# Attention and experts on one core: attention as one written order of pieces, sub-blocks of 24 queries, v in 16 transfers a batch

## The chip, the core and the metric

The kernel runs on one core of a Trainium2 chip. The core has a matmul engine (PE; its weight loads are shown apart as PEld), three engines for elementwise work (DVE, ACT, POOL), a queue engine (SP) that issues most transfers, and 16 DMA engines that carry them out. Each engine takes its instructions strictly in the order in which the program gives them. The metric is the device time of one execution in microseconds, the median of the runs.

## What is computed

Eight batches of eight heads go through two attentions, one over the sequence averaged by fours and one over a band of seven keys around each query. Their sum, seen as 4608 rows of 512 numbers, goes through a layer of eight experts, of which each row takes one.

```python
q_d, k_d, v_d = (x.reshape(B, H, Sd, 4, D).mean(axis=3) for x in (q, k, v))   # B, H, S, D = 8, 8, 576, 64
out_up = np.repeat(sm_attn(q_d, k_d, v_d), 4, axis=2)
mask = np.abs(pos[:, None] - pos[None, :]) < 4
out_local = softmax(where(mask, scale * q @ k.T, -1e9)) @ v
x = (out_up + out_local).transpose(0, 2, 1, 3).reshape(B * S, H * D)
e_idx = argmax(x @ w_gate + modality_bias[modality_id], axis=1)
out[mask_e] = gate_w * (relu(x[mask_e] @ w1[e]) @ w2[e])                      # for each expert e
```

## The kernel before

**Attention** runs over 32 head pairs (8 batches of 4). For a pair, PE transposes q and k (tile tp, 12 transpositions, L238), ACT and DVE copy them out (qT, kT) and the averages are taken (qd, kd, d). The banded scores are small matmuls (sc, L275): the 576 queries are cut into sub-blocks of SUB = 26 with a window of 32 keys each, four sub-blocks to a row of tiles, so the last sub-blocks are partial or missing (46 of 48 in all for a pair). DVE takes maximum and difference (lm, le), ACT the exponential, POOL the normalization (L306, L317), DVE transposes 32x32 blocks (lt, L309) and ACT copies them into Pw (L312). The averaged attention goes through scd, de, pdt and PdT. The values matmuls (avd L334, avl L344) and the final addition on DVE (L352) write X, which holds a batch's rows.

**Loads.** `load_qk` (L188) fetches q and k for two pairs in eight transfers of 144 KB. `load_v` (L199) fetches the windows of v for a whole batch in 23 transfers, one for each sub-block over all eight heads; the first has 29 rows, the last 7, the others 32. `load_vg` (L213) fetches v again for averaging, once for each pair, and POOL averages it (L221, L222). All go through SP's queue in program order; vw has two buffers, so a batch's v waits until the values matmuls two batches back have read theirs.

**Router.** After each batch PE computes the logits (lg, lgt), DVE chooses the expert and the place of each row, POOL scatters the entries (tab, L445, 4 or 5 transfers a batch) and PE, ACT and SP write the rows to DRAM (xr, R, xs; L459, L460, L462). The scatters of the batches after the fifth come after the attention loop.

**Experts.** Units of 256 rows: entries and rows are gathered (tg, xg), transposed and split into two parts (xh, xl), as the weights are (whi, wlo, L612, L613), and multiplied (L677, L724). Two units on rows of the first batches start before the router has ended.

**The order.** A loop over steps n (L764) calls, for each n, the loads and `pre` of pair n, `softmax` of pair n-2, `scores` of pair n-1 and `av` of pair n-3. Within what this gives, the scheduler of the build (L934) places each engine's instructions by its own estimates; priorities are raised for the router's last batch. Eighteen dummy matmuls (tile bz, L95) keep PE active, 12 at the start and 6 at step 4.

Of the kernel before, what the change touches and what calls it, by code (L numbers as in the profile page):

```python
# [7 lines left out]
F32 = mybir.dt.float32  # L8
# [14 lines left out]
SUB, WIN = 26, 32  # L23
# [3 lines left out]
KT = PAD + S - 4 + WIN  # L27
# [10 lines left out]
EARLY = 576 * EB  # L38
# [3 lines left out]
LAG = 3  # L42
N0,N1,N2 = (2,3,4)
PV = 0
AN = 2
LEAD = 8
ST = 1
NPW = 3
SP0 = ()
NS1 = 33  # L50
HOLD = 14
NHOLD = 20
HIP = 1
GO = 1
LS = 1
VD = 0
NCE = (2,1,1)
BZ = (0,0,0,0,6)


class Consts:
    def __init__(s, tc, pool, psum):
# [25 lines left out]
        nc.vector.memset(s.mask[64:96, NB - 1, 4 + PAD : WIN], NEG)  # L88
# [8 lines left out]
    def load(s, tc, pool, work, rows, mid, bias, w_gate):  # L97
# [3 lines left out]
        nc.sync.dma_start(s.wg[:, :, 0:NE], w_gate.rearrange("(j p) e -> p j e", p=128))  # L101
        s.mi = rows.tile([128, DM], F32, name="R", bufs=3)[:36, :256].bitcast(I32)
# [41 lines left out]
    def biases(s, tc, pool, work, rows, psum):  # L144
# [11 lines left out]
        t1 = rows.tile([128, DM], F32, name="R", bufs=3)[:, : 36 * NE].rearrange("p (t e) -> p t e", e=NE)  # L156
# [6 lines left out]
class Attention:  # L163
    def __init__(s, tc, ctx, ectx, C, psum, q, k, v):
# [7 lines left out]
        s.QK, s.V, s.VG = {}, {}, {}  # L172
        s.vw = [(s.ld, s.one)[j].tile([128, NB, H, D], F32, name=f"vw{j}", bufs=1) for j in range(2)]
        s.kT = [s.ld.tile([128, KT], F32, name=f"kT{j}", bufs=1) for j in range(2)]
        s.Pw = [s.one.tile([128, 2 * NB, 4, SUB], F32, name=f"Pw{j}") for j in range(NPW)]
        s.clear(0)

    def clear(s, j):

        nc = s.nc  # L180
        if j < 2:
            nc.vector.memset(s.kT[j][:, 0:PAD], 0.0)
            nc.vector.memset(s.kT[j][:, S + PAD :], 0.0)
            nc.vector.memset(s.vw[j][0:32, 0], 0.0)
            nc.vector.memset(s.vw[j][64:96, NB - 1], 0.0)
        (nc.vector if j == 0 else nc.gpsimd).memset(s.Pw[j], 0.0)

    def load_qk(s, b, half):  # L188
# [4 lines left out]
        for g in range(2):  # L193
            for t, src in ((qt, s.q), (kt, s.k)):
                for a in range(2):
                    nc.sync.dma_start(t[:, g, :, a], src[b, 4 * half + 2 * g + a].rearrange("(j p) d -> p j d", j=6))
        s.QK[b, half] = (qt, kt)

    def load_v(s, b):  # L199
        nc = s.nc  # L200
        vd = s.wk.tile([72, H, 2, D], F32, name="vd")
        vw = s.vw[b % 2]
        s.V[b] = (vw, vd)

        for i in range(NB):
            for j in range(4):
                lo = BLK * i + SUB * j - PAD
                k0, k1 = max(lo, 0), min(lo + WIN, S)
                if lo + PAD < S:
                    nc.sync.dma_start(vw[32 * j + k0 - lo : 32 * j + k1 - lo, i],  # L210
                                      s.v[b, :, k0:k1].rearrange("h p d -> p h d"))

    def load_vg(s, b, hp):  # L213
# [725 lines left out]
```

## Time and profile before

| | |
|---|---|
| median of 3 runs | 798.09 us (797.21 to 799.65) |
| profiled execution | 799.32 us, span 797.6 us |
| mean granted clock of PE | 0.927 |
| DMA | 150.00 MB, mean 188 GB/s |
| chain that ended last | issue and DMA of the last output, below 1% of the span |

The profile gives busy time for each engine, the granted clock of PE and the DMA's share over time, and rows in order of time with the idle time ahead of an instruction and what ended it, in brackets. The chain that ended last breaks off after the last output transfers, so the argument has to come from stretches of the span: attention lies in the first 350 us, the experts behind it.

### The profile page before, as it was taken

To read this page: it belongs to the slowest core of one execution; us is meant where nothing else is said; L and a number is where in the kernel's file an instruction comes from. 1 tells how busy PE (TensorE), PEld (TensorE's weight loads), DVE (VectorE), ACT (ScalarE), POOL (GpSimd) and SP (SyncE) were. 2 spreads that over 40 slices of the span, in tenths; PEclk is the share of its full clock that TensorE was granted. 3 is DMA by queue.
4 is the path that set the end of the run, shared out by engine and by line. 5 is a ranking of instruction groups with operands and counts; after the bars stand their busy time and mean duration, and the time that the engine had idled before them with its cause. 6 is when DMAs were issued, how large, how long until landed. Compare 5 with 4: busy or idle time off the path is not lost. (4 is left out here: it accounts for less than half of the span.)

```text
span 797.6 us, 20726 instructions
## 1 busy us (share of the span) xinstructions
PE 739.1 (93%) x8185; PEld 616.6 (77%) x8185; DVE 469.4 (59%) x957; ACT 426.5 (53%) x882; POOL 319.2 (40%) x362
## 2 busy tenths in 40 slices
PE   8488999899989988899799999999999999999995
PEld 5366767576767666778699888999998899999884
DVE  7534757574657667858476555556555555655520
ACT  4534657474747356855466555545555554555520
POOL 5525565665574658323353333233222333222000
PEclk9685989897989679999989999999999999999998
DMA  8769967577868597334889766677666667666500
GB/s 143 149 135 179 202 132 201 104 177 138 209 125 210 98 235 189 110 108 176 283 275 321 253 207 227 213 249 237 229 227 220 216 225 233 224 217 231 186 13 18
DMA packets 205075, 150.00 MB, mean 188 GB/s; under 512 B 132683, under 2 KB 171631, under 8 KB 204976
## 3 DMA queue, kind: packets, MB, share of 16 engines
q1 hardware_dynamic: 196720, 129.43, 59.5%
q0 software_dynamic: 8256, 19.22, 6.8%
q8 instruction: 65, 1.06, 0.6%
q14 instruction: 34, 0.28, 0.2%
HBM read 129.40 MB, written 19.47 MB: 187 GB/s over the span
## 5 line engine op out<-in xcount | busy, mean ns | idle before, releaser
L613 DVE TENSOR_TENSOR wlo<-raw,whi 128x1024 fp32r<-128x1024 f32 x130 | 160.2, 1245 | 130.4 <-ACT whi L612 120.7
L612 ACT CAST whi<-raw 128x1024 fp32r<-128x1024 f32 x130 | 134.7, 1049 | 120.2 <-PE l L677 54.3
L677 PE MATMUL l<-xh,whi 128*128 128x256 f32 x488 | 138.8, 286 | 0.7 <-ACT xh L660 0.7
L677 PE MATMUL l<-xh,wlo 128*128 128x256 f32 x488 | 138.4, 284 | 0.0
L677 PE MATMUL l<-xl,whi 128*128 128x256 f32 x488 | 138.3, 284 | 0.0
L728 POOL DMA_INDIRECT out_dram<-o,tg x37 | 40.9, 1105 | 173.3 <-ACT o L727 127.7
L724 PE MATMUL l<-wlo,hh 128*128 128x512 f32 x256 | 100.4, 393 | 0.0
L724 PE MATMUL l<-whi,hl 128*128 128x512 f32 x256 | 100.4, 393 | 0.0
L724 PE MATMUL l<-whi,hh 128*128 128x512 f32 x256 | 98.7, 397 | 0.0
L677 PEld LDWEIGHTS l<-xh,whi 128*128 128x128 f32 x488 | 93.3, 192 | 2.5 <-ACT xh L660 1.1
L677 PEld LDWEIGHTS l<-xl,whi 128*128 128x128 f32 x488 | 93.4, 191 | 0.6
L677 PEld LDWEIGHTS l<-xh,wlo 128*128 128x128 f32 x488 | 93.3, 191 | 0.2 <-issue 0.2
L275 PEld LDWEIGHTS sc<-kT,qT 64*26 64x26 f32 (+1 forms) x2944 | 40.7, 104 | 36.6 <-issue 27.3
L275 PE MATMUL sc<-kT,qT 64*26 64x32 f32 (+1 forms) x2944 | 60.7, 199 | 8.9 <-issue 8.4
L626 POOL DMA_INDIRECT tg<-tab,midx x33 | 38.1, 1154 | 75.3 <-DMA out_dram<-o,tg 69.5
L680 DVE SCALAR_TENSOR_TENSOR hl<-l,hh 128x512 fp32r<-128x512 f32 x72 | 49.3, 685 | 24.8 <-ACT hh L679 24.8
L312 ACT COPY Pw<-lt 32x312 f32<-32x312 f32 x128 | 57.7, 451 | 10.4 <-DVE lt L309 8.3
L636 POOL DMA_INDIRECT xg<-xs,tg x37 | 43.3, 1170 | 47.6 <-DMA tg<-tab,midx 29.7
L679 ACT ACTIVATE hh<-l 128x512 fp32r<-128x512 f32 x72 | 42.8, 594 | 32.4 <-PE l L677 29.2
L724 PEld LDWEIGHTS l<-whi,hl 128*128 128x128 f32 x256 | 48.1, 188 | 10.7 <-issue 0.5
L724 PEld LDWEIGHTS l<-wlo,hh 128*128 128x128 f32 x256 | 48.0, 188 | 10.8
L724 PEld LDWEIGHTS l<-whi,hh 128*128 128x128 f32 x256 | 48.1, 188 | 10.6 <-issue 0.5
(203 smaller groups left out, 1444.1 us busy)
## 6 DMA issues: line engine op xcount, KB each, us to landing
raw<-in_moe_w_dram SPq DMA_DIRECT2D x152, 512.0 KB
vw<-in_v_dram SPq DMA_DIRECT2D x168, 64.0 KB
qt<-in_q_dram SPq DMA_DIRECT2D x64, 144.0 KB
kt<-in_k_dram SPq DMA_DIRECT2D x64, 144.0 KB
vg<-in_v_dram SPq DMA_DIRECT2D x32, 288.0 KB
xs<-R SPq DMA_DIRECT2D x36, 256.0 KB
xg<-xs,tg POOLq DMA_INDIRECT x37
out_dram<-o,tg POOLq DMA_INDIRECT x37
```

The costliest lines, as they stand in the source:

```text
L275: nc.tensor.matmul(p[32 * j : 32 * j + q1 - q0, i, :], qT[r, q0:q1], kT[r, q0 : q0 + WIN], start=False, stop=(i == NB - 1), skip_group_che ...
L312: nc.scalar.copy(Pw[r, :, j, :SUB], eT[r, :, :SUB])
L612: nc.scalar.copy(hi, raw)
L613: nc.vector.tensor_tensor(lo, raw, hi.bitcast(F32), op=ALU.subtract)
L626: nc.gpsimd.indirect_dma_start(out=T[:, h, :], out_offset=None, in_=s.tab[:, :], in_offset=bass.IndirectOffsetOnAxis(ap=idx[:, u, h : h + ...
L636: s.gathered = nc.gpsimd.indirect_dma_start(out=R[:, h, :], out_offset=None, in_=s.xs[:n, :], in_offset=bass.IndirectOffsetOnAxis(ap=T[:, ...
L677: nc.tensor.matmul(p[:, f, :], a[:, k, fs], x[:, k, :], start=(k == 0 and i == 0), stop=(k == 3 and i == 2))
L679: nc.scalar.activation(hh[:, 2 * c : 2 * c + 2, :], p, AF.Relu)
L680: nc.vector.scalar_tensor_tensor(hl[:, 2 * c : 2 * c + 2, :], p, 0.0, hh[:, 2 * c : 2 * c + 2, :].bitcast(F32), op0=ALU.max, op1=ALU.subtract)
L724: nc.tensor.matmul(p, a[:, f, hs], x[:, f % 2, :], start=(f == 0 and i == 0), stop=(f == 7 and i == 2))
L728: nc.gpsimd.indirect_dma_start(out=s.out[:, :], out_offset=bass.IndirectOffsetOnAxis(ap=T[:, h, 0:1], axis=0), in_=o, in_offset=None, boun ...
```

## The change

- All pieces of attention and of the router's work for the first seven batches become methods for one engine each. A table, PHASE, gives each piece a time in units of a pair's period (W0 at 11.2 for a batch's last piece); all calls are sorted by pair or batch number plus that time and written out in that order, under a manual schedule in which the build keeps the order as written.
- SUB is 24, so 24 sub-blocks cover the 576 queries exactly. A batch's windows of v are loaded in four parts of two heads, each in four transfers of 32 rows by 12 blocks; the transfers of a part are calls in the sorted order. Windows may now reach into the neighbouring head, where the band mask leaves nothing.
- q and k for two pairs come in four transfers instead of eight, except the first. Heads are paired two apart, with the matching order in the router's weights and the row copies. vg has three buffers and is loaded three pairs ahead.
- The six dummy matmuls at step 4 are gone. Normalization is on POOL for all pairs. The 64 columns of an even batch that belong to the next row block are kept in a tile `late` and copied by POOL.
- The scatters of every batch but the last stand in the sorted order, one call each. The expert weights' loading and splitting are separate calls. The last batch's router and the experts are scheduled by the build, as before.

```diff
-SUB, WIN = 26, 32
+SUB, WIN = 24, 32
-LAG = 3
-BZ = (0,0,0,0,6)
+PHASE = {
+    "tpq1": 0.0047, "tpk1": 0.0434, "qT1": 0.3244, "kT1": 0.4158, "tpq0": 0.4432, "qT0": 0.5686, "tpk0": 0.7338,
...
+}
...
-        for i in range(NB):
-            for j in range(4):
-                lo = BLK * i + SUB * j - PAD
-                k0, k1 = max(lo, 0), min(lo + WIN, S)
-                if lo + PAD < S:
-                    nc.sync.dma_start(vw[32 * j + k0 - lo : 32 * j + k1 - lo, i],
-                                      s.v[b, :, k0:k1].rearrange("h p d -> p h d"))
+        for j in (0, 2, 1, 3):
+            lo = S * H * b + SUB * j - PAD
+            n0, n1 = NB * 2 * part, NB * 2 * part + NB * 2
...
+            nc.sync.dma_start(vw[32 * j : 32 * j + 32, n0:n1],
+                              vf[lo + n0 * BLK : lo + n1 * BLK].rearrange("(n x) d -> x n d", x=BLK)[:32])
...
+            for nm, p in P.items():
+                f, i = (nm[:-1], int(nm[-1])) if nm[-1].isdigit() and nm not in ("ch1", "ch2") else (nm, 0)
+                if f in batch:
+                    for b in range(B - 1):
+                        call(4 * b + p, getattr(ro, parts.get(f, f)), b, i)
+                else:
+                    for n in range(N):
+                        call(n + p, values if f == "X" else getattr(at, parts.get(f, f)), n, i)
+            for b in range(B):
+                if b + 1 < B:
+                    for j in range(4):
+                        call(4 * b - 1 + used + 0.3 + 0.4 * j, at.load_v, b + 1, j)
+            for h in range(2, N // 2):
+                call(2 * h - 3 + last + 0.25, at.load_qk, h // 2, h % 2)
+            for n in range(3, N):
+                call(n - 3 + P["vt"] + 0.25, at.load_vg, n)
...
+            calls.sort(key=lambda x: x[:2])
+            with tc.manual_schedule():
+                for x in calls:
+                    if x[0] < free:
+                        x[2](*x[3])
```

Where instructions move is shown at three places. First SP's queue in mid-attention, around the load of v for an even batch, before:

```order
L196 DMA kt<-in_k_dram 96x6x64 x2
L210 DMA vw_153<-in_v_dram 29x8x64
L210 DMA vw_153<-in_v_dram 32x8x64 x4
L215 DMA vg<-in_v_dram 72x2x512
L210 DMA vw_153<-in_v_dram 32x8x64 x17
L210 DMA vw_153<-in_v_dram 7x8x64
L215 DMA vg<-in_v_dram 72x2x512
L462 DMA xs<-R 128x512 x2
L196 DMA qt<-in_q_dram 96x6x64 x2
L196 DMA kt<-in_k_dram 96x6x64 x2
```

and after the change, the load for an even batch as well:

```order
L230 DMA vw_153<-in_v_dram 32x12x64 x4
L236 DMA vg<-in_v_dram 72x2x512
L209 DMA qt<-in_q_dram 96x12x64 x2
L209 DMA kt<-in_k_dram 96x12x64 x2
L230 DMA vw_153<-in_v_dram 32x12x64 x8
L559 DMA xs<-R 128x512
L230 DMA vw_153<-in_v_dram 32x12x64 x4
L236 DMA vg<-in_v_dram 72x2x512 x2
L209 DMA qt<-in_q_dram 96x12x64 x2
```

The block of 23 v transfers with one vg in it has become groups of four and eight, with vg, q, k and a store of rows between them.

Second POOL's queue where a batch's entries are scattered (tab) in mid-attention, before (vt and vd average v, le and de are normalized, d and kd average k):

```order
L253 TENSOR_TENSOR kd<-d_3857 128x72x2
L445 DMA tab<-ig,si 36864x2 x2
L221 TENSOR_TENSOR vt<-vg 72x512
L445 DMA tab<-ig,si 36864x2 x3
L306 TENSOR_TENSOR le<-le,zr 128x384
L317 TENSOR_TENSOR de<-de,zr 128x432
L221 TENSOR_TENSOR vt<-vg 72x512
```

and after:

```order
L564 DMA tab<-ig,si 36864x2
L357 TENSOR_TENSOR le<-le,zr 128x384
L250 TENSOR_TENSOR vd<-vt 72x256
L564 DMA tab<-ig,si 36864x2
L243 TENSOR_TENSOR vt<-vg 72x512
L564 DMA tab<-ig,si 36864x2
L285 TENSOR_TENSOR d_3138<-kT_156 128x288
L361 TENSOR_TENSOR de<-de,zr 128x432
L290 TENSOR_TENSOR kd<-d_3138 128x72x2
L357 TENSOR_TENSOR le<-le,zr 128x384
```

The five scatters around one vt stand ahead of the normalization before; after the change each scatter has other work on at least one side, and the normalization comes between them.

Third PE's queue within a pair in mid-attention, before (sc are the banded scores, scd and avd belong to the averaged attention, avl are the values, xr the router's rows):

```order
L275 MATMUL sc<-kT_155,qT 26x32 x20
L334 MATMUL avd<-PdT,vd 64x144 x2
L344 MATMUL avl<-Pw_159,vw_154 64x104 x6
L459 MATMUL xr<-ident,X 128x128 x4
L334 MATMUL avd<-PdT,vd 64x144 x2
L459 MATMUL xr<-ident,X 128x128 x4
L238 MATMUL tp<-ident,qt 128x96 x3
L275 MATMUL sc<-kT_155,qT 26x32 x12
L275 MATMUL sc<-kT_155,qT 4x32
L238 MATMUL tp<-ident,qt 128x96 x3
L344 MATMUL avl<-Pw_159,vw_154 64x104 x4
L344 MATMUL avl<-Pw_159,vw_154 64x78 x2
```

and after:

```order
L258 MATMUL tp<-ident,kt 128x96 x3
L304 MATMUL sc<-kT_156,qT 24x32 x48
L393 MATMUL avd<-PdT,vd 64x144 x4
L258 MATMUL tp<-ident,qt 128x96 x3
L258 MATMUL tp<-ident,kt 128x96 x3
L331 MATMUL scd<-kd,qd 64x144 x6
L408 MATMUL avl<-Pw_157,vw_153 64x96 x12
L258 MATMUL tp<-ident,qt 128x96 x3
```

Before, scores, values and transpositions of several pairs are mixed in small pieces that differ from pair to pair; after the change each piece is whole and the sequence repeats from pair to pair.

656 lines of the change are left out of this document (350 added, 306 removed), and 11 rows, old and new, of the table PHASE.

## Prediction

> **What bounds the kernel now.** I start with the page's busy shares and clock row.
>
> ```profile
> PE 739.1 (93%) x8185; PEld 616.6 (77%) x8185; DVE 469.4 (59%) x957; ACT 426.5 (53%) x882; POOL 319.2 (40%) x362
> PEclk9685989897989679999989999999999999999998
> ```
>
> TensorE is busy 93% of the span, and from the twentieth slice on, in the experts, it is full at full clock. The change leaves the experts' instructions as they are, so what can move is the first 350 us, where the clock row falls to 5 and 6 again and again. The table of 20 us stretches shows how (from: to, length; busy us and number of instructions of PE, PEld, DVE, ACT, POOL; granted clock; DMA share; GB/s):
>
> ```profile
> 120.00:140.00 20.00, 19.13 (x394) 14.24 (x392) 14.70 (x50) 13.66 (x41) 11.50 (x14) 1.00 0.78 205
> 140.00:160.00 20.00, 16.64 (x269) 12.14 (x265) 10.62 (x32) 10.12 (x29) 12.80 (x17) 0.83 0.55 97
> 160.00:180.00 20.00, 17.99 (x421) 13.74 (x417) 15.38 (x48) 14.55 (x48) 12.13 (x16) 1.00 0.79 185
> 180.00:200.00 20.00, 18.64 (x274) 13.41 (x275) 9.40 (x25) 8.29 (x27) 11.81 (x15) 0.75 0.70 132
> 200.00:220.00 20.00, 19.84 (x390) 14.65 (x390) 13.83 (x49) 13.84 (x42) 10.50 (x14) 1.00 0.85 214
> 220.00:240.00 20.00, 17.41 (x275) 12.16 (x274) 11.05 (x35) 9.00 (x27) 13.31 (x17) 0.83 0.66 122
> 240.00:260.00 20.00, 19.35 (x429) 14.38 (x429) 14.15 (x47) 13.70 (x45) 10.30 (x13) 1.00 0.85 209
> 260.00:280.00 20.00, 19.29 (x227) 12.91 (x226) 12.41 (x41) 7.55 (x22) 13.70 (x17) 0.66 0.56 100
> ```
>
> Good and bad stretches alternate, one of each to a batch. The good ones (120, 160, 200, 240) hold 394+421+390+429 = 1634 matmul records in 80 us, 20.4 a us, with PE busy 76.3 of 80 and the clock at 1.00. The bad ones hold 1045, 13.1 a us, at 0.66 to 0.83, and there the DMA moves 97 to 132 GB/s instead of about 200. What a head pair costs comes from one longer stretch, first all instructions, then those on tile tp, of which PE has 12 for each pair:
>
> ```profile
> 100.00:260.00 160.00, 147.40 (x2740) 107.76 (x2739) 99.63 (x310) 93.97 (x289) 94.13 (x117) 0.90 0.73 162
> ```
> ```profile
> 100.00:260.00 160.00, 29.34 (x198) 19.83 (x198) 14.90 (x34) 13.33 (x34) 0.90 0.73 162
> ```
>
> 198/12 = 16.5 pairs in 160 us: **9.70 us a pair**, 166 records each. At the good stretches' 20.4 a us a pair would be 8.14 us. DVE, ACT and POOL have 6.0, 5.7 and 5.7 us of work a pair: none is near the bound. So what makes the bad half? The transfer queue's rows in order of time, and its waits:
>
> ```profile
> 12.80 15.05 SPq L210 DMA_DIRECT2D vw<-in_v_dram  x23
> 28.73 0.87 SPq L196 DMA_DIRECT2D qt<-in_q_dram  x2
> 39.80 15.22 SPq L210 DMA_DIRECT2D vw<-in_v_dram  x21
> ```
> ```profile
> 226.79 15.21 SPq L210 DMA_DIRECT2D vw<-in_v_dram  x23
> 242.10 0.98 SPq L215 DMA_DIRECT2D vg<-in_v_dram  x1
> 261.39 0.42 SPq L215 DMA_DIRECT2D vg<-in_v_dram  x1
> ```
> ```profile
> SPq L210 <- PE avl L344: 19.7, 9, 7.6
> ```
>
> The 23 v transfers of a batch hold the queue about 15.2 us, 0.66 us each for 64 KB, the rest of a batch's transfers 19.7 us more (242.10 to 261.81), and v also waits up to 7.6 us for the values matmuls that free its buffer, with q and k of later pairs queued behind it. 15.2 + 19.7 us and waits of a few us are the batch's 38.8 us (four times 9.70): **the in-order queue sets the period**, not an engine. And v is slow on its own account:
>
> ```profile
> 2.00:13.00 11.00, 10.26 (x169) 6.35 (x167) 8.79 (x33) 2.88 (x9) 6.60 (x19) 1.00 1.29 208
> 14.00:28.00 14.00, 9.03 (x274) 6.67 (x271) 11.27 (x34) 11.79 (x42) 5.55 (x8) 0.94 0.45 102
> ```
>
> With q and k queued the DMA gave 208 GB/s at a share of 1.29; with v queued without a gap, 102 at 0.45. [...]
>
> PE pays for the queue directly and through POOL:
>
> ```profile
> 34.20 1.19 PE L238 MATMUL tp<-ident,qt 96*128 96x96 f32 x6 [9.38 <-DMA qt<-in_q_dram]
> 42.81 2.74 PE L95 MATMUL bz<-dummy 128*128 128x512 bf16 x6
> 62.38 1.19 PE L238 MATMUL tp<-ident,qt 96*128 96x96 f32 x6 [6.51 <-DMA qt<-in_q_dram]
> ```
> ```profile
> 225.58 0.24 PE L268 MATMUL sc<-mask,identb 128*128 128x192 bf16 x1 [2.50 <-DVE le L279]
> ```
> ```profile
> 216.87 1.01 POOL L445 DMA_INDIRECT tab<-ig,si  x1 [0.74 <-DVE si L440]
> 223.17 0.97 POOL L445 DMA_INDIRECT tab<-ig,si  x1 [0.30 <-issue]
> 224.17 0.84 POOL L306 TENSOR_TENSOR le<-le,zr 128x384 f32<-128x384 f32 x1
> ```
>
> At 34.20 and 62.38 PE had waited 9.38 and 6.51 us for q. At 225.58 it had waited 2.50 us for the scores' subtraction on DVE: POOL's normalization (224.17) stood behind five scatters in a block from 216.87 on, and the later DVE work behind that.
>
> **The change, part by part.** *The start.* Sizes are in the page's section 6, k's like q's:
>
> ```profile
> vw<-in_v_dram SPq DMA_DIRECT2D x168, 64.0 KB
> qt<-in_q_dram SPq DMA_DIRECT2D x64, 144.0 KB
> vg<-in_v_dram SPq DMA_DIRECT2D x32, 288.0 KB
> ```
>
> The first transfer PE runs dry on is q for pair 4. After the change there stand ahead of it, in KB: q and k of the first four pairs, 16x144 = 2304; vg, 3x288; v, 16x96 (32 rows of 12 blocks of 64 numbers); some 60 for the router; and pair 4's two q transfers themselves, which now bring two pairs at once, 288 each. That is 5340 KB, 5.47 MB. At 208 GB/s from 2 us on it is there at 28.3 us, against 34.20. PE's work up to there is done at about 25 us as before, so a wait of some 3 us stays and the clock falls; I charge 3 us for that and for the six dummy matmuls (2.74 us at 42.81) that go: their loss cannot cost more than the half clock did after 62.38, and their absence gains at most 2.74. Pairs 4 and 5 at the period below: pair 6 starts at 28.3+3+17 = 48.3 instead of 62.38. Its q is behind k of pair 4, the table's fill, two vg and four v, 2.46 MB with itself, 11.8 us, so it is there at 40 and nothing waits. **Gain 14.1 us.**
>
> *The period.* v goes in pieces of a quarter batch between q, k and vg, each due when its buffer is free, so nothing stands behind a wait. What the queue needs a batch: 19.7 us as before, plus v. v is bounded by 1.57 MB at 208 GB/s, 7.6 us, and by the old pace per byte, 15.2 us x 1536/1416 KB = 16.5 us: 27 to 36 us. I take the lower end, near which q and k run, since all transfers but the run's first and last are now 32 full rows, with no more 29 and 7 rows in every batch; q and k come in half as many transfers with the same bytes. PE needs 4x8.14 = 33 us and becomes the bound. To 8.14 us I add 0.35 for waits of a strict order, from these rows:
>
> ```profile
> L460 ACT COPY R<-xr 128x512 f32<-128x512 f32 x36 | 20.3, 589 | 15.8 <-PE xr L459 8.7 <-PE scd L286 2.2 <-PE tp L238 1.7
> L388 ACT COPY LT<-lg 128x256 f32<-128x256 f32 (+1 forms) x16 | 6.4, 398 | 17.3 <-PE lg L386 17.2
> ```
>
> In one pair of each four two R and two LT copies now stand ahead of the copies that the values matmuls wait for: 2x589+2x398 = 2.0 us, of which I let a quarter of ACT's slack (8.1-5.7 = 2.4 us a pair) take 0.6, since the rest of the slack lies elsewhere in the pair; 1.4/4 = 0.35. Together **8.5 us**. The scores' 46 blocks become 48 (4 records of 166, at most 0.2 us a pair), the values matmuls are 96 instead of 104 wide (8% of 24 records, about -0.1): nothing, with ends of -3 and +5 us over the run. POOL gains the copies of 64 leftover columns, four in all, and the first two pairs' normalizations; it has 2.8 us of slack a pair. The scatters, now one at a time, no longer make a block, so the stall at 225.58 goes; last in line is then PE itself. In the last batch SP's reading of the early experts' numbers stands between two pieces of v, with the rest of v, xs and vg behind it; v is wanted three periods later, 25 us, which covers that. The row copies' new pattern and three more small loads at the start I cost at nothing: ACT and SP have the slack named. How far pairs run:
>
> ```profile
> L238 PE MATMUL tp<-ident,qt x192: 243/246/422, 6.0 to 309.6; 96*128 96x96 f32 x192
> ```
> ```profile
> 351.68 0.71 PE L344 MATMUL avl<-Pw,vw 128*64 128x104 f32 x12
> ```
>
> The last q transposition stands at 309.6; from pair 6 on 25.4 periods, 9.73 us each. At 8.5: 48.3 + 25.4x8.5 = 264.2. **Gain 31.3 us there, 45.4 in all.**
>
> *The end of attention.* From 309.6 to the last values matmul (351.68) are 42 us, in which the first expert's work is mixed in before and after. The order hardly differs there, so I cost it at nothing, between -6 (less waiting in the drain) and +8 (weights of the first expert late). After it the routing of the last batch, scatters, reading of the table and gather follow one another as before; PE runs dry at the end of that chain:
>
> ```profile
> 60.00:80.00 20.00, 17.52 (x210) 12.33 (x210) 8.51 (x22) 8.84 (x25) 11.32 (x14) 0.51 0.95 179
> 392.00:400.00 8.00, 2.99 (x12) 1.88 (x11) 4.37 (x5) 4.61 (x7) 4.41 (x4) 0.68 0.93 313
> ```
>
> 3.0 us of 8 are busy there. That gap moves with the chain. The sum: 799.3 (the profiled execution; span 797.6) - 45.4 = **754 us**; the runs' median (798.1) is 1.2 us lower than that execution, which is inside the rounding of these terms.
>
> **The rivals.** *A, v keeps its pace per byte.* Then the queue binds at 36 us a batch, 9.0 us a pair: 25.4x0.5 = 13 us more and 2 at the start, 769. For it: the 15.2 us may be issue cost; against: 0.45 share.
>
> *B, PE runs without waits.* 76.3/80 of 8.14 is 7.8 us a pair: 754 - 25.4x0.7 = 736.
>
> *C, half the gain stays in the order.* Each wait now blocks all behind it on its engine; at 9.4 us a pair: 777. Against: in the good stretches the old order, as fixed per engine as this one, needed 8.14.
>
> *D, slower.* The written order makes PE wait 2.5 us or more for ACT's copies in every second pair; after such a wait (225.58) the clock fell, and the pace was the bad stretches' 166/13.1 = 12.7 us. 754 + 12.7x4.2 = 807. It decides from 754 + 45.4, a mean period of 10.3 us. After 62.38 such a cold stretch held to 80 (clock 0.51). [...]
>
> ```profile
> 200.00:220.00 20.00, 5.39 (x36) 3.38 (x36) 2.01 (x5) 2.35 (x6) 1.00 0.85 214
> 220.00:240.00 20.00, 1.79 (x12) 1.46 (x12) 1.51 (x4) 0.84 (x2) 0.83 0.66 122
> ```
>
> The stretch with 36 of tp's transpositions ran at 1.00, the one with 12 at 0.83.
>
> That the change does not do what it says is no case of its own: the rows shown with the change have v in pieces and the scatters apart.
>
> **How the numbers follow.** Forecast (8.15 to 8.85 us a pair, 745 to 763): 0.56. A 0.17, B 0.11, C 0.11, D 0.05. The range leaves out D, most of C and the far end of B: 738 to 776. Within 0.3% of 798.1, which is about what a measurement can tell, ends only C with other losses: 0.03. Faster 0.92, slower 0.05.
>
> **What would show it.** A clock row at 9 up to the experts; 8.5 us between a tile's transpositions of one pair and the next; no v burst with the DMA at 0.45; q for pair 4 awaited until 28 us and no wait at pair 6; the last values matmul at 306. The queue never idle and PE waiting for q or vg means A; a clock of 0.5 in mid-attention, with PE waiting for ACT, D. I am wrong altogether if PE's waits per pair come to 2 us.

## The result and the profile after

The changed kernel takes **763.74 us** (median of 4 runs, 763.37 to 764.57) against 798.87 us for the kernel before beside it: a ratio of 0.9547, with a 95% interval of 0.9492 to 0.9602. The forecast was 754, with a range of 738 to 776. In the text TensorE is the engine of the rows PE and PEld, VectorE that of DVE, ScalarE that of ACT and GpSimd that of POOL. The profiled execution took 764.05 us, 35.27 less than the profiled one of before. From the page of the changed kernel, the busy shares, the granted clock and the share of the DMA engines over 40 equal slices of the span:

```profile
PE 695.0 (91%) x8307; PEld 599.1 (79%) x8307; DVE 472.6 (62%) x956; ACT 422.2 (55%) x876; POOL 321.7 (42%) x369
PEclk8589998999997999998899999999999999999998
DMA  9999999989987982749797666766676766666500
```

The clock row reads 7 to 9 in all slices but the second, which is at 5. Before, it stood at 5 or 6 in three slices (the second, fourth and fourteenth) and at 7 to 9 in the others, so the page alone shows a small difference; the prediction's "again and again" rests on the stretches of 20 us and not on that row. The DMA row stands at 7 to 9 for the first 15 slices, to 286 us, nearly all of attention. One batch of attention shows both best, from its first v transfer to that of the next batch: from, to and length, then busy us and records of PE, PEld, DVE, ACT, POOL, then clock, DMA share, GB/s. First the kernel before, then the changed one:

```profile
189.50:226.80 37.30, 34.56 (x677) 25.30 (x677) 23.84 (x76) 21.38 (x66) 21.03 (x25) 0.99 0.80 170
```
```profile
168.80:202.40 33.60, 28.44 (x676) 22.16 (x675) 24.80 (x78) 22.12 (x70) 23.69 (x29) 0.98 1.06 194
```

At nearly the same clock (0.99 and 0.98) and the same number of TensorE records (677 and 676) the batch takes 33.6 us instead of 37.3. TensorE is busy 28.44 us instead of 34.56, and it now idles 5.2 us of the batch instead of 2.7. The 6.1 us overstate the gain, since the two stretches do not hold the same mix (20 records of xr and 48 of tp before, 13 and 45 after): over 16 whole pairs, in the table below, TensorE's work falls by 13.9 us, 3.5 a batch. The other engines' work is the same within some 2.7 us, and the DMA engines' share went from 0.80 to 1.06. I had taken the time that TensorE needs for a pair as given; it is not.

The start. TensorE's rows of the changed kernel in order of time (start, duration, then in brackets the wait before and what ended it), and those of the transfer queue:

```profile
30.63 0.29 PE L160 MATMUL mp<-ident,mf 36*128 36x36 f32 x1 [9.44 <-DVE mf L158]
39.73 0.74 PE L258 MATMUL tp<-ident,qt 96*128 96x96 f32 x3
53.63 0.47 PE L258 MATMUL tp<-ident,qt 96*128 96x96 f32 x3
```
```profile
11.91 9.53 SPq L230 DMA_DIRECT2D vw<-in_v_dram  x16
23.33 2.67 SPq L110 DMA_DIRECT2D wg<-in_moe_w_gate_dram  x4
26.24 0.36 SPq L113 DMA_DIRECT2D R<-in_moe_modality_id_dram  x1
```
```profile
0.00:20.00 20.00, 14.67 (x257) 9.63 (x257) 8.66 (x41) 5.55 (x15) 10.77 (x32) 0.83 1.16 180
20.00:40.00 20.00, 9.38 (x142) 7.05 (x140) 7.63 (x23) 4.91 (x16) 7.22 (x11) 0.50 1.06 164
```

Pair 4 (39.73) no longer waits for its q. But ahead of it stands a single small transposition into mp, the router's modality numbers, and it waits 9.44 us: its load now stands in the queue behind all of the first batch's v, three vg and the four w_gate transfers (26.24), while before the change it stood ahead of v, at 11.55. Pair 6 starts at 53.63 instead of 62.38.

The pace and the end, from the view of tile tp and from TensorE's timeline:

```profile
L258 PE MATMUL tp<-ident,qt x192: 243/246/423, 6.2 to 277.9; 96*128 96x96 f32 x192
```
```profile
309.69 1.21 PE L408 MATMUL avl<-Pw,vw 128*64 128x96 f32 x24
```

The last q transposition stands at 277.9 (before: 309.6), the last values matmul at 309.69 (351.68). From pair 6 on that is (277.9 - 53.63)/25.4 = 8.83 us a pair. Inside attention three waits of TensorE are longer than 2 us:

```profile
98.39 0.75 PE L546 MATMUL xr<-ident,X 128*128 128x128 f32 x3 [4.25 <-issue]
```
```profile
200.08 1.04 PE L408 MATMUL avl<-Pw,vw 128*64 128x96 f32 x19 [3.11 <-issue]
232.23 0.32 PE L295 MATMUL sc<-mask,identb 128*128 128x192 bf16 x1 [5.38 <-DVE le L317]
```
```profile
224.56 0.16 DVE L576 COPY ec<-cp 128x8 f32<-128x8 f32 x1
224.75 1.90 DVE L582 TENSOR_SCALAR eni<-ec 128x8 int32<-128x8 f32 x1
231.82 0.35 DVE L317 TENSOR_TENSOR le<-sc,lm 128x192 f32<-128x192 f32 x1
```

The third is plain. VectorE works through the early experts' table, 21 instructions written in one block (from 224.56 on; one of them, at 224.75, takes 1.90 us), and the scores' subtraction that TensorE waits for stands behind it (231.82). The first two are of another kind: they lie in the middle of a group of equal matmuls (three of four, 19 of 24), and nothing that the profile shows is waited for ("issue").

### The profile page after: what moved, and what is told of

Read it like the earlier page. It is cut to its first block, busy times and chain, and to the rows that moved or that the text cites. A ratio compares the mean times of both kernels' runs of the same rounds, so it can differ in the third digit from the quotient of the medians.

```text
span 762.4 us, 20954 instructions
## 1 busy us (share of the span) xinstructions
PE 695.0 (91%) x8307; PEld 599.1 (79%) x8307; DVE 472.6 (62%) x956; ACT 422.2 (55%) x876; POOL 321.7 (42%) x369
## 5 line engine op out<-in xcount | busy, mean ns | idle before, releaser
L797 DVE SCALAR_TENSOR_TENSOR hl<-l,hh 128x512 fp32r<-128x512 f32 x72 | 49.3, 685 | 23.9 <-ACT hh L796 23.9
L753 POOL DMA_INDIRECT xg<-xs,tg x37 | 40.1, 1083 | 51.1 <-DMA tg<-tab,midx 40.8
L372 ACT COPY Pw<-lt 32x288 f32<-32x288 f32 x128 | 55.0, 430 | 9.5 <-DVE lt L367 7.8
L841 PEld LDWEIGHTS l<-wlo,hh 128*128 128x128 f32 x256 | 48.1, 188 | 10.8
L841 PEld LDWEIGHTS l<-whi,hl 128*128 128x128 f32 x256 | 48.1, 188 | 10.6 <-issue 0.5
L841 PEld LDWEIGHTS l<-whi,hh 128*128 128x128 f32 x256 | 48.1, 188 | 10.2
L408 PE MATMUL avl<-Pw,vw 128*64 128x96 f32 x768 | 44.2, 267 | 10.5 <-ACT Od L398 4.6
L564 POOL DMA_INDIRECT tab<-ig,si x36 | 36.8, 1023 | 38.0 <-DVE mn L649 26.6
```

The lines of the kernel that those rows point to most:

```text
L372: s.nc.scalar.copy(s.Pw[n % NPW][r, :, j, :SUB], s.t["lt", n][r, :, :SUB])
L408: s.nc.tensor.matmul(p[64 * a : 64 * a + 64, c], vw[:, NB * (4 * (hp // 2) + hp % 2 + 2 * a) + k, :], Pw[:, NB * a + k], start=True, stop= ...
L564: i = nc.gpsimd.indirect_dma_start(out=s.tab[:, :], out_offset=bass.IndirectOffsetOnAxis(ap=C.si[:, t : t + 1], axis=0), in_=C.ig[:, t, :] ...
L753: s.gathered = nc.gpsimd.indirect_dma_start(out=R[:, h, :], out_offset=None, in_=s.xs[:n, :], in_offset=bass.IndirectOffsetOnAxis(ap=T[:, ...
L797: nc.vector.scalar_tensor_tensor(hl[:, 2 * c : 2 * c + 2, :], p, 0.0, hh[:, 2 * c : 2 * c + 2, :].bitcast(F32), op0=ALU.max, op1=ALU.subtract)
L841: nc.tensor.matmul(p, a[:, f, hs], x[:, f % 2, :], start=(f == 0 and i == 0), stop=(f == 7 and i == 2))
```

## Experiments

Times are medians with the range of the runs, ratios are to the kernel before in runs of the same chip. That kernel itself gave 797 to 816 us on the chips used, so kernels are compared on one chip where a per cent matters. e1 to e3 and b1 ran on one chip, e4 to d1 on a second, s1 to after_again on a third and v1 on a fourth. The changed kernel itself ran only in its first measurement and on the third; beside the others its 763.74 and 765.52 us are taken, and a gain or loss of half a per cent would not show.

| run | time, us | ratio to before, 95% interval |
|---|---|---|
| the changed kernel | 763.74 (763.37 to 764.57) | 0.9547 (0.9492 to 0.9602) |
| e1_bias_first | 766.77 (762.97 to 770.79) | 0.9552 (0.9468 to 0.9637) |
| e2_early_spread | 764.83 (763.69 to 767.01) | 0.9516 (0.9457 to 0.9575) |
| e3_both | 764.45 (762.73 to 765.57) | 0.9502 (0.9448 to 0.9556) |
| b1_split29 | 799.26 (798.26 to 805.18) | 0.9931 (0.9892 to 0.9970) |
| e4_scheduler | 823.24 (817.99 to 827.79) | 1.0182 (1.0083 to 1.0282) |
| e5_v_block | 771.88 (767.67 to 775.99) | 0.9545 (0.9462 to 0.9628) |
| e6_entries_late | 765.31 (759.19 to 767.39) | 0.9490 (0.9412 to 0.9568) |
| d1_less_v | 763.99 (761.83 to 764.50) | 0.9460 (0.9382 to 0.9537) |
| s1_broken_scores | 765.45 (764.85 to 768.14) | 0.9573 (0.9517 to 0.9628) |
| t1_qk_small | 765.78 (761.59 to 769.85) | 0.9562 (0.9492 to 0.9632) |
| after_again | 765.52 (764.02 to 767.83) | 0.9567 (0.9511 to 0.9624) |
| v1_less_dve | 775.68 (772.64 to 777.18) | 0.9694 (0.9648 to 0.9740) |

The next table is worked out from the TensorE records and clock intervals of each profiled execution. The first four columns cover the 16 pairs from the first q transposition of pair 8 to that of pair 24, where no start and no early expert disturbs: the time, the time in which no matmul ran, the time at half clock, and TensorE's work (busy time, that at half clock counted half). Then the starts of the last q transposition and of the last values matmul, all in us.

| run | pairs 8 to 24 | idle | half clock | work | last tp | last avl |
|---|---|---|---|---|---|---|
| before | 153.7 | 12.2 | 30.7 | 128.3 | 309.6 | 352.2 |
| changed | 140.5 | 18.0 | 17.1 | 114.4 | 277.9 | 310.7 |
| after_again | 136.4 | 15.7 | 17.1 | 112.6 | 278.4 | 311.0 |
| e1 | 139.4 | 15.8 | 23.9 | 112.7 | 277.7 | 309.5 |
| e2 | 144.4 | 18.6 | 23.9 | 113.9 | 280.0 | 311.8 |
| e3 | 141.0 | 13.7 | 34.1 | 111.3 | 280.0 | 311.4 |
| e6 | 140.3 | 13.9 | 27.3 | 113.2 | 273.6 | 306.1 |
| d1 | 134.1 | 13.0 | 13.7 | 114.7 | 275.0 | 308.1 |
| s1 | 135.7 | 9.7 | 13.7 | 119.1 | 276.5 | 309.9 |
| t1 | 137.8 | 15.3 | 20.5 | 113.2 | 278.4 | 311.1 |
| e5 | 141.6 | 17.1 | 27.3 | 113.3 | 285.4 | 318.5 |
| v1 | 144.5 | 21.7 | 27.3 | 110.9 | 288.1 | 320.9 |
| e4 | 164.4 | 12.7 | 37.5 | 134.5 | 338.1 | 377.0 |

The changed kernel, after_again, e1, e2, e3 and e6 have the same code in these 16 pairs, and differ from 136.4 to 144.4: a single execution tells 8 us there, not 2. Their work differs less, from 111.3 to 114.4.

### e1: the router's small loads ahead of v

```diff
+            C.load_bias(tc, work, ro.wk, mid, bias)   # the loads of mi and bb, taken out of C.load
             at.load_vg(0)
             for j in range(4):
                 at.load_v(0, j)
```

> The changed kernel, with the router's modality numbers and biases loaded ahead of the first v instead of behind it. Theory 1 (the 9.44 us wait of the transposition into mp at 30.63, with everything behind it on TensorE, is what the start term lacked): the wait at mp falls under 2 us, pair 4's first transposition starts at 31 to 33 us instead of 39.7, pair 6's at 45 to 48 instead of 53.6, and the time is 755 to 758 us instead of 763.7. Rival (the start is bounded by the bytes that have to arrive): the wait moves to q of pair 4 or to v or vg, over 6 us of it is left, and the time is 761 to 764.

Its TensorE rows:

```profile
32.76 0.71 PE L261 MATMUL tp<-ident,qt 96*128 96x96 f32 x3 [3.30 <-DMA qt<-in_q_dram]
36.08 0.71 PE L261 MATMUL tp<-ident,kt 96*128 96x96 f32 x3 [2.61 <-DMA kt<-in_k_dram]
```

Pair 4 starts at 32.76 instead of 39.73, as theory 1 has it, but waits of 3.30 and 2.61 us for q and k are there now. Pair 6 starts at 50.1, later than the 45 to 48 of theory 1, so 3.5 us are gained; at pair 8 it is 64.1 against 67.0, and the last q transposition stands at 277.7, where it stood without the edit. The time does not fall. The wait was real, but what was saved there was waited for again further on.

### e2, e3, e6: the block on VectorE, and the wait behind it

```diff
-            call(t, first)
+            for i in range(6):                        # early() cut into six pieces
+                call(t - 1.5 + 0.3 * i, first, i)
```

> The changed kernel, with the 28 VectorE instructions of the early experts' table in six pieces 0.3 pairs apart, from 1.5 pairs earlier on, instead of in one block. Theory 1 (this block is the 5.38 us wait of TensorE at 232.23, and the slow clock up to 242 follows from it): the wait is under 2 us, the clock from 220 to 240 is 0.9 or more instead of 0.79, and the time is 754 to 759 us. Rival (VectorE has to do this work anyway, and in pieces it holds up as much): waits of under 1 us each at several places, 762 to 764.

> Both edits of the two runs before together, in the changed kernel. If the two losses are independent and both were on TensorE's path: their gains add up, 746 to 752 us. If something else, such as the transfer queue or the expert weights' stream, takes over as the bound: 755 or more, with new waits for DMA on TensorE.

(The block has 21 instructions, not 28.) The 5.38 us wait for the subtraction is down to 1.21 us in both, and neither is faster. Another wait took its place. From e3, TensorE's row and GpSimd's:

```profile
237.53 1.49 PE L381 MATMUL pdt<-ident,de 128*72 128x128 f32 x6 [3.80 <-POOL de L364]
```
```profile
234.95 0.98 POOL L770 DMA_INDIRECT tg<-tab,eidx  x1 [5.00 <-DVE qd L283]
236.56 0.92 POOL L364 TENSOR_TENSOR de<-de,zr 128x432 f32<-128x432 f32 x1
```

GpSimd's first read of the expert table (tg) waits 5.00 us. The profile names VectorE's qd, which ended just before; but the read also needs what the last scatter wrote, whose issue ended 6.3 us before, at 228.63, and which of the two held it is not shown. The normalization that TensorE needs stands behind it in GpSimd's order (236.56), so TensorE waits 3.80 us. In the changed kernel the same read waited 6.37 us, beside the wait for VectorE's block. e6 puts the reads 0.8 pairs later:

```diff
-                call(t + 0.5 + 0.35 * i, entries, i // 2, i % 2)
-                call(t + 1.85 + 0.35 * i, rows, i // 2, i % 2)
-            call(t + 4.2, split, 0)
+                call(t + 1.3 + 0.35 * i, entries, i // 2, i % 2)
+                call(t + 2.65 + 0.35 * i, rows, i // 2, i % 2)
+            call(t + 4.6, split, 0)
```

> The two edits of e3_both, and GpSimd's reads of the early experts' table and of their rows 0.8 pairs later, behind the time at which the last scatter has landed. Theory 1 (each removed stall had another right behind it, here GpSimd's 5.00 us wait at 234.95 with TensorE's 3.80 us behind it; when that goes too, the sum shows): no wait of TensorE over 2 us from 215 to 245, last q transposition at 268 to 273 instead of 277.9, 752 to 759 us. Rival (something that paces attention as a whole, the transfers or the clock, sets its end, and stalls only move): last q transposition again at 276 to 281, 762 to 766.

Now no wait of TensorE from 215 to 245 is over 2 us, and the profiled execution, the fastest of its four, had its last q transposition at 273.6 and took 759.19 us. The other three took 764.4 to 767.4. On the median it is the rival's number: three named stalls of 9.4, 5.4 and 5.0 us are gone, and the time is what it was.

### b1: the 29-row transfer

In the kernel before:

```diff
-                    nc.sync.dma_start(vw[32 * j + k0 - lo : 32 * j + k1 - lo, i], ...)
+                    for x0, x1 in ((k0, 16), (16, k1)) if k0 > lo else ((k0, k1),):
+                        nc.sync.dma_start(vw[32 * j + x0 - lo : 32 * j + x1 - lo, i], ...)
```

> The kernel before, with the batch's first v transfer, 29 rows, cut into 16 and 13 rows; nothing else. [...] Rival (each transfer holds the queue 0.66 us whatever its rows): 24 transfers hold it 15.9 us, and the time stays at 797 to 801.

Two of its v bursts, and a stretch within the first:

```profile
12.38 13.87 SPq L211 DMA_DIRECT2D vw<-in_v_dram  x24
265.09 12.66 SPq L211 DMA_DIRECT2D vw<-in_v_dram  x24
```
```profile
14.00:28.00 14.00, 9.16 (x274) 6.68 (x271) 11.51 (x35) 12.04 (x43) 5.56 (x8) 0.92 0.52 113
```

The run asks how much of the burst's 15.2 us the transfer of 29 rows costs. The 24 transfers hold the queue 13.87 and 12.66 us, 0.53 to 0.58 each, where 23 held it some 15.2. The share in the burst is 0.52 instead of 0.45. So in these two bursts the first transfer cost 1.3 to 2.5 us. But most of the burst stayed, at some 0.55 us for each of the 24: nearer the rival. The single records of the queue show the cost more plainly: in the kernel before, the transfer right behind the 29 rows held the queue 2.46 to 4.54 us in seven batches of eight (in the second batch it is a vg, 3.71), and in b1 the one behind the 16 rows 0.39 to 0.42. Other transfers took part of that back; the second batch's 23 transfers even held the queue 16.69 us from 34.79. The time falls by 0.7% (0.3 to 1.1).

### e4: the same pieces without the written order

```diff
-            with tc.manual_schedule():
+            with ExitStack():
```

(at both places)

> The changed kernel, same pieces, same transfers, but without the strict order around the sorted calls: the build's scheduler sets each engine's order again. Theory 1 (the gain comes from the transfers: 16 whole v transfers a batch, in quarters, and half as many q and k transfers): about the time of the changed kernel, 760 to 772 us. Rival (the gain comes from the written order): most of it is gone, 785 to 805.

**This is the run that tells the change's parts apart.** With all the new transfers and pieces, but with the build's scheduler in charge, the kernel is 0.8 to 2.8% slower than before: 823 us. The rival holds, and more than it said. TensorE's work from pair 8 to 24 is 134.5 us, more than in the kernel before (128.3), where the written order needs 114.4 for the same matmuls. That is 20.1 of the 23.9 us between the two runs in these pairs. A score run of this execution, broken by transpositions:

```profile
104.58 0.42 PE L304 MATMUL sc<-kT,qT 64*24 64x32 f32 x28
104.93 0.47 PE L258 MATMUL tp<-ident,kt 96*128 96x96 f32 x3
105.33 0.71 PE L304 MATMUL sc<-kT,qT 64*24 64x32 f32 x58
105.97 0.47 PE L258 MATMUL tp<-ident,qt 96*128 96x96 f32 x3
```

Record by record, at full clock in these pairs and counted at most up to the next one's start, a score record takes 16 ns in e4 and 11 in the changed kernel, one of tp 122 and 107, of lg 117 and 70, of avl 57 and 49: the same instructions last longer when they are mixed. e4 gives the order of the transfers back to the scheduler as well. The opposite run, 23 transfers and sub-blocks of 26 queries under the written order, was not made. Nor was any of the other parts undone alone (the dummies, the pairing of heads, the third vg buffer), so what these are worth is not known.

### e5 and t1: the transfers' part

```diff
-                        call(4 * b - 1 + used + 0.3 + 0.4 * j, at.load_v, b + 1, j)
+                        call(4 * b - 1 + used + 0.3, at.load_v, b + 1, j)
```

> The changed kernel, with the four quarters of a batch's v called one right after the other, at the place of the first, instead of 0.4 pairs apart. Theory 1 (spreading v between q, k and vg is part of the gain, since 16 transfers in a row hold the queue some 10 us): waits of TensorE or GpSimd for q, k or vg come back, 768 to 780 us. Rival (it is the number of v transfers that counts, and not where they stand): 762 to 766.

With v in one block the waits for loads are back on TensorE:

```profile
56.51 0.54 PE L258 MATMUL tp<-ident,kt 96*128 96x96 f32 x3 [2.64 <-DMA kt<-in_k_dram]
```
```profile
157.81 0.71 PE L258 MATMUL tp<-ident,kt 96*128 96x96 f32 x3 [2.14 <-DMA kt<-in_k_dram]
```

At 771.88 it is 7 us over the two others on its chip that keep v apart (e6 at 765.31 and d1 at 763.99, which have other edits), and the last q transposition stands 7.5 us later: theory 1, at some 1% of the time. The other half of the new transfers, q and k for two pairs at once, is undone by t1:

```diff
-        for g in range(2) if (b, half) == (0, 0) else (slice(0, 2),):
+        for g in range(2):
```

> The changed kernel, with q and k in twice as many transfers of half the size (144 KB each, as before the change). Theory 1 (the transfer queue's time per transfer is still near the bound): some 70 more transfers of 0.3 to 0.4 us each, 3 us a batch more on the queue, waits of TensorE for q or k come back, 770 to 780 us. Rival (the queue has slack once the order no longer puts v ahead of everything): 762 to 767.

The time stays (765.78 beside 765.52 for after_again). But a wait on ScalarE has grown from 3.3 and 4.6 us in the two executions of the changed kernel, by the view of waits from 60 to 300 us (total, times, longest):

```profile
ACT R L553 <- DMA xs<-R: 13.0, 4, 4.8
```

The copy of finished rows waits for a free buffer R, which is free when the store of an older row has landed; that store stands in the same queue as all loads.

### d1: fewer bytes of v

```diff
+            w = 32 if b < 2 else 8
-            nc.sync.dma_start(vw[32 * j : 32 * j + 32, n0:n1], ...[:32])
+            nc.sync.dma_start(vw[32 * j : 32 * j + w, n0:n1], ...[:w])
```

> The changed kernel, with v's window transfers of batches 2 to 7 carrying 8 of their 32 rows: the same number of transfers, a quarter of the bytes, so the values of those batches are computed from old rows, and the time is that of the same instructions with some 0.9 of 6.3 MB per batch less to move. Theory 1 (the DMA engines, at a share of 0.9 to 1.2 all through attention, pace it, directly or through late fetches of instructions): last q transposition at 265 to 272 instead of 277.9, fewer waits of TensorE in the middle of a run of matmuls, 750 to 758 us. Rival (order and clock pace it): 277 to 280, 762 to 766.

A batch of it, as above:

```profile
163.00:197.50 34.50, 31.08 (x688) 24.41 (x686) 25.72 (x78) 23.28 (x72) 23.54 (x29) 0.93 0.78 150
```

The share is 0.78 instead of 1.06, the batch takes 34.5 us instead of 33.6 (at a clock of 0.93 instead of 0.98), and the time is 763.99. From pair 8 to 24 this execution is the shortest of all (134.1), 2.3 us below the range of the unchanged code, and only one wait over 0.9 us is left there; by the end nothing of that remains. The bytes do not set the time: the rival's number. Nor does the time that the queue takes to issue: from pair 8 to 24 its records fill 123.0 of 140.5 us in the changed kernel and 94.3 of 134.1 in d1.

### s1 and after_again: what a broken run costs

In s1 the scores of a pair, 48 matmuls, come in four runs of 12, with avd and two groups of tp between:

```diff
-"sc0": 1.8420, "sc1": 1.8495,
+"sc0": 1.8420, "sc1": 1.8845, "sc2": 2.0048, "sc3": 2.0435,
```

> The changed kernel, with the 48 score matmuls of a head pair written in four runs of 12, with the values' coarse matmuls and two groups of three transpositions between the runs, instead of in one; same instructions, same transfers. Theory 1 (a good part of the gain is that the written order keeps TensorE's runs whole: in the trace of before a run of scores costs some 0.08 us more for each break, and the transpositions behind it some 0.10): TensorE's busy time at full clock from pair 8 to 24 rises from 114 us to 121 to 124, and the time is 771 to 780 us. Rival (breaks cost nothing, or TensorE's idle time of 18 us there takes them up): the time stays at 762 to 767.

> The changed kernel as it is, once more beside the two others on the same chip: 762 to 766 us by its first measurement. It says how far one execution's stalls, at fixed places in the program or not, differ from another's: if the stops in the middle of TensorE's runs (4.25 us at 98.39, 3.11 us at 200.08) come from late fetches of instructions behind full transfers, they stand at the same places in the program with other lengths.

TensorE's rows, first of the changed kernel, with the run whole, then of s1, both at full clock (a score matmul has two records):

```profile
145.35 1.01 PE L304 MATMUL sc<-kT,qT 64*24 64x32 f32 x96
146.28 0.71 PE L393 MATMUL avd<-PdT,vd 72*64 72x144 f32 x8
146.92 0.47 PE L258 MATMUL tp<-ident,qt 96*128 96x96 f32 x3
147.23 0.41 PE L258 MATMUL tp<-ident,kt 96*128 96x96 f32 x3
```
```profile
109.68 0.37 PE L305 MATMUL sc<-kT,qT 64*24 64x32 f32 x24
109.98 0.47 PE L258 MATMUL tp<-ident,qt 96*128 96x96 f32 x3
110.38 0.37 PE L305 MATMUL sc<-kT,qT 64*24 64x32 f32 x24
```

From start to start the whole run takes 146.28 - 145.35 = 0.93 us, 0.23 for a quarter, and three transpositions that other transpositions follow 0.31. In s1 a quarter takes 0.30, and three transpositions that scores follow 0.40. A break costs some 0.07 where the scores stop and, behind transpositions, 0.09 where they start again. The table agrees: work rises from 112.6 to 119.1 us in 16 pairs with three breaks each, 0.14 us a break (0.10 against the first execution's 114.4). So the first half of theory 1 is shown, though 119.1 is short of its 121 to 124. The second is not: idle falls from 15.7 to 9.7, and the time is the same, 765.45 beside 765.52. **TensorE's work is not what sets the changed kernel's pace.**

after_again has its stops in the middle of a run at the same places of the program as the first execution (98.39 and 200.08), with other lengths:

```profile
95.61 0.55 PE L546 MATMUL xr<-ident,X 128*128 128x128 f32 x3 [2.07 <-issue]
```
```profile
196.29 1.86 PE L408 MATMUL avl<-Pw,vw 128*64 128x96 f32 x19 [4.55 <-issue]
```

The second, after 5 of 24 values matmuls, is also in e1 (1.96 us), e2 (2.03) and e6 (2.28). It is 0.80 us in d1, with fewer bytes on the way, but 0.72 in e3, with all of them.

### v1: less work on VectorE

```diff
-        s.nc.vector.tensor_reduce(dd, s.t["qT", n]...)
+        if n < 2:
+            s.nc.vector.tensor_reduce(dd, s.t["qT", n]...)
```

> The changed kernel, with the sums of four q columns (0.74 us of VectorE a pair) computed for the first two pairs only and these used for all later ones, so the coarse scores of the others come from old sums: 30 x 0.74 = 22 us less work on VectorE, which after TensorE is the busiest engine (some 14.6 of 20 us from 60 to 200), everything else as it was. Theory 1 (VectorE's order paces a pair in attention, so that work taken from TensorE, from the transfers or from the single stalls comes back as waiting): pairs 8 to 24 take 130 us or less instead of 136 to 141, the last q transposition stands at 262 to 270 instead of 278, and the time is 748 to 758 us. Rival (latencies between the engines, late fetches and the half clock that follows idle time pace it, and no engine's work): pairs 8 to 24 stay at 135 to 141, the time at 762 to 767.

Neither theory: with 22 us of work taken away the kernel is 10 to 12 us slower than the changed one (775.68 against 763.74 and 765.52). ScalarE's waits from 60 to 300 us, one of them in its timeline, and the queue's row for the store:

```profile
ACT R L555 <- DMA xs<-R: 17.5, 5, 7.6
```
```profile
197.13 0.58 ACT L555 COPY R<-xr 128x512 f32<-128x512 f32 x1 [7.60 <-DMA xs<-R]
197.61 0.30 ACT L400 ACTIVATE Od<-avd 128x144 f32<-128x144 f32 x1
```
```profile
181.69 6.38 SPq L231 DMA_DIRECT2D vw<-in_v_dram  x8
189.00 3.12 SPq L561 DMA_DIRECT2D xs<-R  x2
```

The row copy waits 7.60 us for the store of an older row. The queue took 6.38 us for eight v transfers and then 3.12 for two stores, and only when they had landed was a buffer free. Behind the copy in ScalarE's strict order stands the copy Od (197.61) that TensorE's values matmuls wait for: 6.54 us there, 4.42 at 125.13. In all 17.5 us in five waits, against 3.3 in the changed kernel's first execution and 4.6 in the second. The copy of rows, the stores and the loads form a loop through the queue. Why this edit lengthened it is not shown; the edit also gives qd two fixed buffers, whose share was not measured.

## Why the prediction was right, and where its steps were wrong

In the profiled execution the 45.4 us of the forecast became 35.3. The time is inside the range, but just outside the 745 to 763 us that the forecast itself covered. By its terms:

- **The start: 14.1 forecast, 8.75 measured** (62.38 to 53.63). The step that failed is "three more small loads at the start I cost at nothing": the loads, and with them the transposition into mp, had been moved behind v, and I had counted only the bytes ahead of q. e1 shows 3.5 of the missing 5.4 us. The rest is the rate: 208 GB/s was taken, and 180 and 164 GB/s stand in the rows of the first 40 us; in e1 q landed at 32.8 instead of 28.3.
- **The period: 31.3 forecast, 22.9 measured**: 25.4 x (9.73 - 8.83). The size is near, the make-up is not. I built 8.5 from 8.14 of TensorE and 0.35 of waits. From pair 8 to 24 the table gives 140.5/16 = 8.78 a pair: work 114.4/16 = 7.15, idle 18.0/16 = 1.13, and the rest, 0.5, is what half clock added. "At the good stretches' 20.4 a us a pair would be 8.14" took the good stretches of before for what the matmuls need. They held broken runs: over the 16 pairs the work was 128.3 us before, 8.0 a pair, and 114.4 after.
- **"The in-order queue sets the period, not an engine"** fell as the sole cause. The queue's records fill 126.5 of 153.7 us in these pairs before and 123.0 of 140.5 after, so the queue has hardly less to do; TensorE has. The new transfers without the order give 823 us (e4). With the 29 rows split, the v burst still held the queue 13.87 and 12.66 of some 15.2 us (b1), so that transfer was the smaller part of it. The 7.6 us a batch for v ("I take the lower end") are shown by no run: that full rows bring it was my estimate, and in the changed kernel the 16 transfers of a batch hold the queue 11.7 to 13.2 us (four batches from 99.38 on). That v stands apart is worth some 1% under the written order (e5), and the size of the q and k transfers nothing (t1).
- **The end: nothing forecast, within -6 and +8; 3.6 gained.** From the last q transposition to the last values matmul 31.8 us instead of 42.1 (10.3 gained). From there on 6.7 were lost, and the rows where TensorE runs dry, first of the changed kernel, then of before, show the places:

```profile
357.78 0.94 PE L775 MATMUL xt<-ident,xg 128*128 128x128 f32 x4 [3.35 <-DMA xg<-xs,tg]
365.05 1.12 PE L775 MATMUL xt<-ident,xg 128*128 128x128 f32 x4 [2.31 <-DMA xg<-xs,tg]
```
```profile
395.22 1.11 PE L658 MATMUL xt<-ident,xg 128*128 128x128 f32 x4 [2.90 <-DMA xg<-xs,tg]
397.76 1.11 PE L658 MATMUL xt<-ident,xg 128*128 128x128 f32 x4 [1.43 <-DMA xg<-xs,tg]
```

  From the last values matmul to the first row here are 48.1 us instead of 43.5, and a further wait of 2.31 us for gathered rows stands at 365.05, where before the last such wait was that of 397.76.

That the forecast held is in good part luck: losses and gains that it did not have cancelled to 10 us, and its reason for the period was not the one that the runs show. Of the rivals, A (9.0 us a pair, 769) came nearest in time, nearer than the forecast, but its cause is excluded: the 16 transfers of the first v held the queue 9.53 us and the blocks of e5 10.1 to 14.0, not 16.5, and a quarter of v's bytes (d1) and twice as many q and k transfers (t1) leave the time as it is. B had its condition half met: TensorE's work is below even B's 7.8, and the waits took the difference. C's strict order did cost waits, on top of less work: idle went from 0.76 to 1.13 us a pair. D did not come: its point was a mean period of 10.3 us, and after pair 4 the clock was never at half for more than 10.2 us together.

Of what would show it: the absence of a v burst at share 0.45 came true, and the clock row nearly (9 in 11 of the first 16 slices). 8.5 a pair and the last values matmul at 306 came out as 8.83 and 309.7. The wait for pair 4's q was not there, since another hid it.

**What stays open** is what sets 8.5 to 9 us a pair now. It is not TensorE's work (s1), not v's bytes nor the queue's time to issue (d1), not the number of q and k transfers (t1), and not the three named stalls (e1, e2, e3, e6), since each could be changed without the time following. VectorE's work was not cleanly tested, since v1 ran into the row stores. Left are a loop through several engines and the queue, like that of the row stores, late instructions (below), and the half clock that follows idle time (after 77 of 77 steps with TensorE busy under half, below); no run separates these. Open too is how much of the gain is TensorE's smaller work by itself: s1 puts 4.7 to 6.5 of the 13.9 us back and costs nothing, and e4 changes the work and the placing of all waits at once.

## What to carry to other kernels

Where a written order lets every engine wait for every other, count the records that a whole stretch needs at full clock before taking a "good" stretch of the old trace as an engine's need: an order that keeps runs of small matmuls whole lowered that need by 15% (134.5 us in e4, 114.4 in the changed kernel). A single long wait in such a kernel is a poor target, for three of them were removed and nothing was gained; test first whether added work on the engine that waits costs anything. And when a load moves, look for the smallest consumer of it in a strict order: one transposition of 36 columns held TensorE for 9.4 us.

## What the runs showed of the hardware that was not expected

**Late instructions.** The long "issue" waits coincide with packets of a queue named instruction, 16 KB each. By the DMA view of the changed kernel from 93 to 99 us, share of 16 engines:

```profile
q1 hardware_dynamic: 3785, 1.13, 98.7%
q8 instruction: 1, 0.02, 1.5%
```

The data queue alone has 98.7% there. From the records of that queue and TensorE's, time of each packet, how long it took, and how many instructions TensorE had started since the one before:

```
 85.64 us  0.98 us  289        187.37 us  1.72 us  291
 95.44 us  1.42 us  386        197.40 us  1.17 us  384
 99.97 us  2.57 us   19        202.43 us  0.93 us   56
```

A packet comes for every 250 or so (67 packets for 16801 instructions), so I take the queue to be TensorE's. Where TensorE stopped, at 94.1 and 196.9 us, it had come only after 386 and 384, and the stop ended 1.5 us after it had landed. That full data queues delay the packet is not shown: the stop at the second place is as short in e3 (0.72 us), with all bytes, as in d1 (0.80), and the time of the request is in no trace.

**The clock.** It was granted in steps of 3.41 us: its intervals in attention last 3.4, 6.8, 10.2, 27.3 us and other multiples. Over the 14 executions of this study, by steps up to 400 us and TensorE's busy share in each:

```
busy share   steps at full clock   followed by half    steps at half clock   followed by full
below 0.50          77                   77                    63                    0
0.50 - 0.72        112                   50                    34                    0
0.72 - 0.90        236                   26                    42                    0
over 0.90          835                    0                   226                  151
```

A step of the changed kernel, with the one behind it (their borders are rounded, hence 0.99 and 0.51):

```profile
160.10:163.50 3.40, 2.55 (x106) 2.07 (x92) 2.83 (x10) 3.31 (x12) 3.21 (x5) 0.99 1.10 165
163.50:166.90 3.40, 3.40 (x37) 2.79 (x34) 1.47 (x4) 0.52 (x1) 3.40 (x5) 0.51 0.64 106
```

TensorE was busy for 75% of the first one (2.55 of 3.40 us), with no wait over 0.9 us, and the next was spent at half clock. So here a step with short waits alone was followed by one at half clock, as were 26 of 236 that were busy for 72 to 90%. At half clock only steps that were over 90% busy were followed by full clock, 151 of 226.

**Broken runs.** A break in a run of scores cost 0.10 to 0.14 us in s1. What that time is made of no run here shows.
